# Swapping two VectorE instructions at the end of the output phase: the next attention's second scaling ahead of the last gated product

## The chip, the cores and the metric

The kernel runs on one core of a Trainium2 chip. The metric is device time in microseconds (us). PE is TensorE (matmul), DVE is VectorE, ACT is ScalarE, POOL is GpSimd, SP issues DMAs. Each engine has an instruction queue of its own; engines wait for each other through semaphores.

## The reference

Eight batches of linear attention (8 heads, 576 tokens, head dimension 64) are followed by a gated feed-forward layer over all 4608 tokens (model width 512, hidden width 1536):

```
kv  = k^T v                      # per head, 64 x 64
o   = q kv
x   = o / sqrt(mean(o*o) + 1e-6) * g_norm          # heads side by side: 512 wide
hid = gelu(x @ w_gate) * (x @ w_val)               # 1536 wide
out = x + sigmoid(x @ w_res) * (hid @ w_out)
```

## The kernel before

Tokens are worked through in nine blocks. Blocks 0 to 7 hold 512 tokens of one batch each; block 8 holds the 64 remaining tokens of each of the eight batches. A block has a **gate/value phase** (`x @ w_gate`, `x @ w_val`, GELU, product) and an **output phase** (`hid @ w_out`, sigmoid gate, sum with x). The attention of batch `b` is computed inside the phases of earlier blocks: for b = 3 to 7 its raw output o is made and scaled across the output phase of block b-2 and the gate/value phase of block b-1. So what is "next" in the output phase of block m is the attention of batch m+2.

There is no scheduler. Every engine executes in the order in which the Python code issues its instructions. Two tables place the attention's pieces between the feed-forward's: `amid_gv` (pieces behind a given word of the gate/value order) and `amid_out` (pieces at a given place of the output phase, called by `aside(key)`).

**The output phase.** Large products are cut into quadrants and computed with seven products in place of eight (Strassen-Winograd), so each phase is a chain of seven matrix products with sums between them. In `others()` of `out_by_products` the last five products are issued by `prod` (L518, 12 matmuls each) into the PSUM banks w_A, w_E, w_A, w_F, w_A. `sub` (L481) makes the sums on DVE. `pf` (L701) multiplies a finished quarter by its gate into the result tile `osb`: the quarter from w_E, the one from w_F, the one that was set aside (on POOL), and last the one from w_A. That last `pf((1, 0), w["A"])` is the **last gated product**; it is the last reader of the bank w_A.

**The scaling.** `a_t(b, i)` (L348) multiplies part i of the raw attention output (a PSUM bank `op`) by the inverse norms `ny` and writes the fp16 tile `t`. It is the last reader of that `op` bank. There are four such parts per batch. Part 0 is placed at key "11" (at "01" in block 1), ahead of the last gated product; part 1, the **second scaling**, is the first item of `aside("end")`. For blocks 2 to 5 it is the only item there; for block 1 two sums over tokens (`ts`, L481, third and fourth of `token_sums`) follow it. Parts 2 and 3 are placed behind the words 1v and Fv of the following gate/value group (in block 2's group: Fv and cv). All of this is on DVE.

**The gate/value phase that follows.** `gv_group` works through a string of words. The first group of blocks 2 to 6 uses

```
1g 1v Eg 5g 6g Ev 5v dg 6v dv Fg 2g Fv 2v 7g g11 7v cg 3g cv 3v h11 g12 4g g21 h12 4v g22 h21 h22
```

A digit is a product on PE (L949, 4 matmuls), g for the gate and v for the value side. Products 1, 6, 7 and 4 go into the bank A of their side, 5 and 3 into F, 2 into E. `E` (`seed`, L959, ACT) copies A, as product 1 left it, into bank E. `d` (`keep`, L963, ACT) copies F, as product 5 left it, to SBUF. `F` and `c` (`plus`, L970, DVE) add d to A. `g11` and the like are GELUs (L980, ACT), `h11` and the like the products with the value side (L986, DVE, for 22 POOL). In the second group of a block the order is `1g 1v Eg 5g Ev 5v dg 6g dv 6v Fg 2g Fv 2v 7g ...`.

**Who holds which bank.** `banks_of` assigns the eight PSUM banks. In the first group of the next block, bank E of the value side (Ev) is the bank that was w_A, so the seed `Ev` waits for the last gated product. Bank F of the gate side (5g) is the bank of part 0 of the attention output; bank F of the value side (5v) is the bank of part 1, so product 5v waits for the second scaling. Within the group: 6v overwrites what the seed `Ev` reads, so it waits for that copy; 7g and 7v write onto A behind 6g and 6v, so they wait for the DVE sums `Fg` and `Fv`, which read A; 4g and 4v wait likewise for `cg` and `cv`.

Of the kernel before, what the change touches and what calls it, by code (L numbers as in the profile page):

```python
# [18 lines left out]
def kernel(  # L19
# [343 lines left out]
    def row_times_g(blk, jj, eng):  # L363
        eng.tensor_tensor(out=t_t[blk][:, jj, :], in0=t_t[blk][:, jj, :], in1=g16, op=ALU.mult)  # L364
# [109 lines left out]
    def b_of(i, j):  # L474
        return wo16[:, (i - 1) * NFH : i * NFH, (j - 1) * CH : j * CH]

    def a_of(blk, i, j):
        return hids[blk][:, (j - 1) * NFH : j * NFH, (i - 1) * PR : i * PR]

    def sub(eng, out_, in0, in1, op=ALU.subtract):  # L480
        eng.tensor_tensor(out=out_, in0=in0, in1=in1, op=op)  # L481
# [29 lines left out]
    def s_last(blk):  # L511
        sub(nc.vector, hid_sums[3], a_of(blk, 1, 2), hid_sums[1])

    def prod(ps, a, b, start, es=(0, 1)):

        for e in es:
            for f in range(NFH):
                nc.tensor.matmul(  # L518
                    ps[:, e - es[0], :],
                    lhsT=a[:, f, e * P : (e + 1) * P],  # L520
                    rhs=b[:, f, :],
                    start=(start and e == es[0] and f == 0),
                    stop=(f == NFH - 1),
                    skip_group_check=True,
                )
# [76 lines left out]
    def res_and_attn(blk):  # L602
        return WHOLE <= blk and blk + 2 < B
# [4 lines left out]
    def out_by_products(blk, banks, amid):  # L608
# [3 lines left out]
        def aside(ahead_of):  # L612
            for f in amid.get(ahead_of, ()):
                f()
# [82 lines left out]
        def part(jj):  # L697
            return slice(None), slice(2 * jj[0], 2 * jj[0] + 2), slice(jj[1] * CH, (jj[1] + 1) * CH)

        def pf(jj, src, eng=nc.vector):  # L700
            eng.tensor_tensor(out=res_all[part(jj)], in0=th_all[part(jj)], in1=src, op=ALU.mult)  # L701
# [10 lines left out]
        def others():  # L712


            prod(w["A"], s_[1], wo_t[:, 1], False)
            aside("F")
            sub(nc.vector, w["F"], w["A"], w["d"], ALU.add)
            if res_and_attn(blk):
                s_last(blk)
            aside("00")  # L720
            prod(w["E"], a_of(blk, 1, 2), b_of(2, 1), False)
            if not whole(blk + 1):
                pf((0, 0), w["E"])
            aside("22")
            prod(w["A"], s_[2], wo_t[:, 2], False)
            c22 = res_all[part((1, 1))]
            sub(nc.vector, c22, w["A"], w["d"], ALU.add)
            if whole(blk + 1):
                pf((0, 0), w["E"])
            aside("01")  # L730
            prod(w["F"], s_[3], b_of(2, 2), False)
            pf((0, 1), w["F"])
            aside("11")
            prod(w["A"], a_of(blk, 2, 2), wo_t[:, 3], False)
            if whole(blk + 1):
                pf((1, 1), c22, nc.gpsimd)
                pf((1, 0), w["A"])
                aside("end")
            else:
                pf((1, 1), c22)  # L740
                pf((1, 0), w["A"])
            if blk + 1 == WHOLE or blk + 1 == LAST[0]:
                nc.gpsimd.tensor_copy(out=hold, in_=x_sums[blk + 1][0:1, 3, 1, 1, 0:1])
            if blk == LAST[0]:
                nc.gpsimd.tensor_copy(out=hold, in_=s_[3][0:1, 0, 0:1])
            for j in range(NJ):
                row_times_g(blk, j, nc.gpsimd)
            if blk == LAST[0]:
                for p in range(B // 2):
                    row_times_g(B, p, nc.gpsimd)  # L750
            rows_behind()

        def rows_behind():

            for i in (1, 0):
                at_word(blk + 1, 0, "h22", lambda i=i: fin((i, i)), lambda i=i: fin((i, 1 - i)))
                at_word(blk + 1, 1, "h22", lambda i=i: store(i))
# [637 lines left out]
    def whole(blk):  # L1395

        return WHOLE <= blk < B - 1
# [249 lines left out]
```

## Time and profile before

| | us |
|---|---|
| median of three runs (lowest to highest) | 320.42 (320.38 to 320.46) |
| span of the profiled execution, first to last instruction | 319.6 |
| PE busy | 309.5 |
| DVE busy | 275.2 |
| ACT busy | 210.8 |
| POOL busy | 188.0 |

The page gives only the span of the profiled execution; the median lies 0.8 us above it, and a change of the span is read as a change of the time. The granted PE clock is full in all 40 slices (mean 0.999). A matmul is shown with a modelled duration of 0.27 us, while the next one starts 0.109 us later, so four matmuls of a product appear as 0.60 us and the next product starts after 0.44 us. DVE and ACT instructions that follow each other without a wait overlap a little in the record: a 0.68 us DVE instruction is followed after 0.60 us, a 0.57 us ACT copy after 0.49 us. Times in the trace are microseconds from the span's start. The output phases of blocks 1 to 5 end, on PE, near 92.0, 124.4, 156.9, 189.4 and 222.2 us.

### The profile page before, as it was taken

How to read it: one execution, taken by the hardware profiler on the slowest of the kernel's cores; microseconds unless marked ns; L12 is line 12 of the kernel's file. 1: busy time of each engine (PE TensorE's matmuls, PEld its weight loads, DVE VectorE, ACT ScalarE, POOL GpSimd, SP SyncE). 2: the span in 40 equal slices, each digit the busy share in tenths (PEclk: the TensorE clock that was granted, in tenths of full speed). 3: DMA queues.
4: the chain of work that ended last, by engine and by line, in shares of the span. 5: the costliest groups of instructions: out<-in, count | busy, mean ns of one | idle time of the engine just before them, and what ended most of it. 6: DMA issues, size and time to landing. Idle time of an engine off the chain costs nothing.

```text
span 319.6 us, 7753 instructions
## 1 busy us (share of the span) xinstructions
PE 309.5 (97%) x3039; PEld 245.6 (77%) x3039; DVE 275.2 (86%) x488; ACT 210.8 (66%) x385; POOL 188.0 (59%) x248
## 2 busy tenths in 40 slices
PE   7899989999999999999999999999999999999993
PEld 2544755444788888888888888888888888888882
DVE  5886979799898999989998999899988777897774
ACT  4763675456848794879587858795767467736770
POOL 2873350573769479756875887517761375396332
PEclk9999999999999999999999999999999999999999
DMA  7999999799994699479947694800340003000204
GB/s 253 328 192 202 195 203 196 162 153 189 171 118 82 199 138 97 82 216 128 105 84 215 88 145 71 226 6 0 68 148 2 0 3 132 2 2 40 93 0 131
DMA packets 77253, 38.89 MB, mean 122 GB/s; under 512 B 42146, under 2 KB 74914, under 8 KB 77218
## 3 DMA queue, kind: packets, MB, share of 16 engines
q0 software_dynamic: 39280, 17.17, 42.7%
q1 hardware_dynamic: 37360, 20.71, 24.8%
q10 hardware_dynamic: 578, 0.52, 0.5%
q8 instruction: 23, 0.38, 0.5%
q14 instruction: 12, 0.10, 0.1%
HBM read 38.80 MB, written 9.44 MB: 151 GB/s over the span
## 4 chain that ended last, share of the span: by engine, by line
PE 84%; DMA 11%; SPq 1%; POOL 1%; DVE 1%; issue 0%; DVEq 0%
PE Ag L949 12%; PE Av L949 11%; PE wA L518 11%; PE Fv L949 6%; PE Fg L949 6%; DMA wg<-in_moe_w_gate_dram 5%; DMA wo<-in_moe_w_out_dram 5%; PE rA L569 4%; PE gps L413 3%; PE fps L450 3%; PE vps L413 3%; PE Ev L949 3%; PE Eg L949 3%; PE wD L518 3%; PE wF L518 3%; PE wE L518 3%
## 5 line engine op out<-in xcount | busy, mean ns | idle before, releaser
L986 POOL TENSOR_TENSOR hid<-ge,c 128x512 f16<-128x512 f16 x22 | 25.6, 1164 | 37.9 <-ACT ge L980 37.9
L518 PEld LDWEIGHTS <-hid_s 128*128 128x128 f16 x384 | 37.6, 98 | 4.4
L949 PEld LDWEIGHTS <-wsv 128*128 128x128 f16 x352 | 34.1, 98 | 5.2 <-issue 1.1
L949 PEld LDWEIGHTS <-wsg 128*128 128x128 f16 x352 | 34.4, 98 | 4.0
L364 POOL TENSOR_TENSOR t<-t,g 128x512 f16<-128x512 f16 x32 | 37.1, 1188 | 0.0
L705 POOL TENSOR_TENSOR osb<-osb,t 128x512 f32<-128x512 f32 x28 | 34.1, 1246 | 0.0
L959 ACT COPY Eg<-Ag 128x512 f32<-128x512 f32 x22 | 12.8, 584 | 27.9 <-PE Ag L949 27.9
L518 PEld LDWEIGHTS <-hid 128*128 128x128 f16 x288 | 28.2, 98 | 3.5
L949 PEld LDWEIGHTS <-wg 128*128 128x128 f16 x264 | 25.8, 98 | 3.2
L949 PEld LDWEIGHTS <-wv 128*128 128x128 f16 x264 | 25.8, 98 | 3.0
L949 PE MATMUL Av<-ts,wsv 128*128 128x256 f16 x176 | 26.4, 272 | 0.1
L949 PE MATMUL Ag<-ts,wsg 128*128 128x256 f16 x176 | 26.4, 273 | 0.0
L970 DVE TENSOR_TENSOR Fg<-Ag,d 128x512 f32<-128x512 f32 x22 | 15.3, 697 | 11.0 <-ACT d L963 8.1
L261 DVE TENSOR_REDUCE ss<-sq 128x8 f32<-128x512 f32 x32 | 20.5, 679 | 2.4 <-ACT sq L256 2.4
L401 ACT ACTIVATE ge<-gps 128x512 f16<-128x512 f32 x20 | 11.9, 598 | 15.6 <-PE gps L413 13.6
L518 PE MATMUL wA<-wo_ts,hid_s 128*128 128x256 f16 x168 | 20.6, 273 | 0.0
L980 ACT ACTIVATE ge<-Eg 128x512 f16<-128x512 f32 x22 | 13.2, 598 | 9.9 <-PE Eg L949 9.9
L980 ACT ACTIVATE ge<-c 128x512 f16<-128x512 f32 x22 | 13.8, 627 | 7.7 <-DVE c L970 7.7
L413 PE MATMUL vps<-xT,wv 128*128 128x512 f16 x72 | 18.5, 379 | 0.4 <-DMA wv<-in_moe_w_val_dram 0.3
L348 DVE TENSOR_TENSOR t<-op,ny 128x512 f16<-128x512 f32 x28 | 18.4, 684 | 0.5 <-POOL ny L322 0.4
L970 DVE TENSOR_TENSOR c<-Ag,d 128x512 f32<-128x512 f32 x22 | 15.2, 689 | 3.9 <-PE Ag L949 3.8
L413 PE MATMUL gps<-xT,wg 128*128 128x512 f16 x72 | 18.5, 379 | 0.0
(220 smaller groups left out, 851.0 us busy)
## 6 DMA issues: line engine op xcount, KB each, us to landing
out_dram<-osb SPq DMA_DIRECT2D x14, 512.0 KB, 3.4
qraw<-in_q_dram POOLq DMA_DIRECT2D x7, 512.0 KB, 6.5
k<-in_k_dram POOLq DMA_DIRECT2D x7, 512.0 KB, 8.4
v<-in_v_dram POOLq DMA_DIRECT2D x7, 512.0 KB, 10.4
wg<-in_moe_w_gate_dram POOLq DMA_DIRECT2D x2, 512.0 KB, 9.5
wo<-in_moe_w_out_dram POOLq DMA_DIRECT2D x2, 512.0 KB, 13.6
out_dram<-osb SPq DMA_DIRECT2D x4, 256.0 KB, 3.8
wv<-in_moe_w_val_dram POOLq DMA_DIRECT2D x3, 256.0 KB, 8.5
```

Source lines behind the costliest of these rows:

```text
L261: nc.vector.tensor_reduce(out=out_, in_=sqs.pop((b, i)), op=ALU.add, axis=mybir.AxisListType.X)
L348: nc.vector.tensor_tensor(out=t, in0=o, in1=scale, op=ALU.mult)
L364: eng.tensor_tensor(out=t_t[blk][:, jj, :], in0=t_t[blk][:, jj, :], in1=g16, op=ALU.mult)
L413: nc.tensor.matmul(ps[:, j0 * P : j1 * P], lhsT=w[:, cc, :], rhs=xT_t[blk][:, j0:j1, cc, :], start=(cc == 0 and j0 == 0), stop=(cc == NP - ...
L518: nc.tensor.matmul(ps[:, e - es[0], :], lhsT=a[:, f, e * P : (e + 1) * P], rhs=b[:, f, :], start=(start and e == es[0] and f == 0), stop=( ...
L569: nc.tensor.matmul(out_[:, e, :], lhsT=x_[:, e, cc, :], rhs=w_[:, cc, :], start=(first and e == 0 and cc == 0), stop=(cc == 1), skip_group ...
L705: nc.gpsimd.tensor_tensor(out=res_all[of], in0=res_all[of], in1=t_t[blk][of], op=ALU.add)
L949: nc.tensor.matmul(out_[:, r, :], lhsT=lhsT, rhs=rhs, start=(first and r == 0 and c == 0), stop=(c == 1), skip_group_check=True,)
L959: nc.scalar.copy(out=tile_of("E", u), in_=ps["A", u])
L970: nc.vector.tensor_tensor(out=dst, in0=ps["A", u], in1=sb["d", u], op=ALU.add)
L980: nc.scalar.activation(out=ge[q], in_=source(q, "g"), func=AF.Gelu)
L986: eng.tensor_tensor(out=dst, in0=ge[q], in1=source(q, "v"), op=ALU.mult)
```

## The change

In `others()`, the branch for blocks whose next block is one of 2 to 6, `aside("end")` is moved ahead of the last gated product:

```
             if whole(blk + 1):
                 pf((1, 1), c22, nc.gpsimd)
+                aside("end")
                 pf((1, 0), w["A"])
-                aside("end")
             else:
```

The branch is taken in the output phases of blocks 1 to 5. DVE's order there becomes, for blocks 2 to 5, scaling 0, scaling 1, gated product of w_A, scaling 2 (before: scaling 0, gated product, scaling 1, scaling 2). For block 1 it becomes gated product of w_F, scaling 1, two `ts` sums, gated product of w_A (before: gated products of w_F and w_A, scaling 1, two `ts` sums). No instruction is added or removed, and the order on PE, ACT, POOL and SP is the same in both kernels. Product 2v of the following group gets a semaphore wait of its own for the gated product; before, that was already covered by the wait of product 5v. A few waits for POOL move to a neighbouring GELU on ACT.

More of the change, by code (lines that the diff above doesn't have):

```diff
@@ L736, in others @@
                 pf((1, 1), c22, nc.gpsimd)
+                aside("end")
                 pf((1, 0), w["A"])
-                aside("end")
             else:
```

## The prediction

> **What bounds the kernel now.** I read the page's busy times first, then the chain of work that ended last, then the waits of each engine, then the timeline of all engines from 124.3 to 130.7 us, where block 2's output phase ends and block 3's gate/value phase starts.
>
> ```profile
> PE 309.5 (97%) x3039; PEld 245.6 (77%) x3039; DVE 275.2 (86%) x488; ACT 210.8 (66%) x385; POOL 188.0 (59%) x248
> PE 84%; DMA 11%; SPq 1%; POOL 1%; DVE 1%; issue 0%; DVEq 0%
> ```
>
> PE bounds it, and behind the opening the chain stays on PE product after product: whatever delays PE between 90 and 230 us delays the end by as much, and nothing behind it waits for another engine long enough to give that back. In the waits of ACT the row that matters is the seed Ev waiting for the gated product.
>
> ```profile
> ACT Ev L959 <- DVE osb L701: 0.5, 3, 0.2
> ```
>
> Now the timeline (start, duration, engine, instruction, idle time before it).
>
> ```profile
> 124.35 0.69 DVE L348 TENSOR_TENSOR t<-op,ny 128x512 f16<-128x512 f32 x1
> 124.96 0.68 DVE L701 TENSOR_TENSOR osb<-th,wA 128x512 f32<-128x512 f32 x1
> 124.99 0.57 ACT L959 COPY Eg<-Ag 128x512 f32<-128x512 f32 x1 [3.54 <-PE Ag L949]
> 125.23 0.60 PE L949 MATMUL Fg<-ts,wsg 128*128 128x256 f16 x4
> 125.55 1.28 DVE L348 TENSOR_TENSOR t<-op,ny 128x512 f16<-128x512 f32 x2
> 125.67 0.60 PE L949 MATMUL Ag<-ts,wsg 128*128 128x256 f16 x4
> 125.72 0.57 ACT L959 COPY Ev<-Av 128x512 f32<-128x512 f32 x1 [0.16 <-DVE osb L701]
> 126.21 0.59 ACT L963 COPY d<-Fg 128x512 f32<-128x512 f32 x1
> 126.29 0.60 PE L949 MATMUL Fv<-ts,wsv 128*128 128x256 f16 x4
> 126.72 0.60 PE L949 MATMUL Av<-ts,wsv 128*128 128x256 f16 x4
> 126.83 0.70 DVE L970 TENSOR_TENSOR Fg<-Ag,d 128x512 f32<-128x512 f32 x1
> 126.92 0.59 ACT L963 COPY d<-Fv 128x512 f32<-128x512 f32 x1
> 127.54 0.70 DVE L970 TENSOR_TENSOR Fv<-Av,d 128x512 f32<-128x512 f32 x1
> 128.03 0.60 PE L949 MATMUL Ag<-ts,wsg 128*128 128x256 f16 x4
> 128.47 0.60 PE L949 MATMUL Av<-ts,wsv 128*128 128x256 f16 x4
> ...
> ```
>
> Three things are to be seen. Product 5v (Fv, 126.29) starts 0.62 us after 6g (125.67) instead of 0.44: it waits for the second scaling, 125.55 + 0.68 = 126.23, so PE loses 0.18 us. DVE runs back to back from 124.35 to 127.5; the product of w_A ended long before DVE came to it (124.14 + 0.38 = 124.52 against 124.96), so moving it fills no idle DVE time, it only trades places. And ACT waits for the gated product before Ev (124.96 + 0.68 = 125.64, Ev at 125.72), with both d copies queued behind Ev, and DVE's Fg and Fv behind the d copies (126.21 + 0.59 = 126.80, Fg at 126.83).
>
> **The change part by part: blocks 2 to 5.** The four boundaries repeat within 0.02 us (Ev at 125.72, 158.26, 190.79 and 223.57), so one is worked and counted four times. Steps used: DVE to the next DVE 0.60; ACT copy to the next 0.49; DVE end to ACT start 0.08 (125.64 to 125.72); ACT end to DVE start 0.03; DVE end to PE start 0.06 (126.23 to 126.29); product to product 0.44.
>
> The second scaling goes to 124.96 and ends at 125.64. Product 5v can start at its own pace, 126.10: 0.18 us won, all of it on PE.
>
> The gated product goes to 125.55 and ends at 126.23. Ev therefore runs 126.31 to 126.88 (now 125.72 to 126.29). No row shows a hand-over from ACT to PE; its nearest rows are 0.06 (DVE to PE) and 0.03 to 0.08 (DVE with ACT), I take 0.06. Product 6v, which overwrites what Ev reads, starts at 126.94 instead of its own pace 126.54: 0.40 lost, against now (126.72) 0.22. Within 0.05 this hand-over decides nothing below.
>
> The d copies follow at 126.80 and 127.28, ending 127.39 and 127.87. Scaling 2 keeps its slot (126.15). DVE's Fg starts at 127.42 instead of 126.83, after 0.6 us of DVE idle; Fv at 128.02 instead of 127.54 (+0.48). Product 7g at its own pace is 128.25 and Fg ends at 128.12: no wait. Product 7v at its own pace is 128.69; Fv ends at 128.70, so 7v starts at 128.76 (now 128.47: +0.29). DVE then runs scaling 3 at 128.62, cg 129.22, cv 129.82 to 130.50; product 4v at its own pace is 130.51, with the hand-over 130.56 (now 130.22: +0.34).
>
> DVE has no idle time to make up its 0.48 before the second group: it is back to back up to that group's Fv, because the remainder's scaling sits there. The row of that Fv and of the 7v behind it, from the timeline of 133.5 to 135:
>
> ```profile
> 133.84 0.68 DVE L970 TENSOR_TENSOR Fv<-Av,d 128x512 f32<-128x512 f32 x1
> 134.58 0.60 PE L949 MATMUL Av<-ts,wsv 128*128 128x256 f16 x4
> 134.78 0.69 DVE L970 TENSOR_TENSOR c<-Ag,d 128x512 f32<-128x512 f32 x1 [0.26 <-PE Ag L949]
> ```
>
> Fv ends at 134.52 and 7v starts 0.06 later: no slack beyond the hand-over. With DVE 0.48 late PE is 0.48 late there. Behind it DVE waits 0.26 us for 7g (and 0.60 us in the third group), so it catches up and nothing more is lost. Sum per boundary: +0.48 us, the 0.18 won already in it. Times four: **+1.92 us**.
>
> **Block 1.** Here three instructions pass the gated product, from the timeline of 91.9 to 99:
>
> ```profile
> 92.42 0.68 DVE L701 TENSOR_TENSOR osb<-th,wA 128x512 f32<-128x512 f32 x1
> 93.01 0.69 DVE L348 TENSOR_TENSOR t<-op,ny 128x512 f16<-128x512 f32 x1
> 93.19 0.57 ACT L959 COPY Ev<-Av 128x512 f32<-128x512 f32 x1
> 93.61 0.42 DVE L481 TENSOR_TENSOR ts<-xT 128x512 f16<-128x512 f16 x1
> ```
>
> Scaling and two sums take 0.60 + 0.34 + 0.34 = 1.28 us, so the gated product runs 93.70 to 94.38. Ev moves from 93.19 to 94.46 and ends at 95.03; 6v moves from 94.19 to 95.09 (+0.90). The d copies end at 95.54 and 96.03, Fg starts at 95.57 (now 94.30), Fv at 96.17 and ends at 96.85. 7v at its own pace would be 96.83, with Fv 96.91 (now 95.93: +0.98). Scaling 2, cg, cv follow; cv ends at 98.65, 4v starts at 98.71 (now 97.68: +1.03). The next group has no remainder scaling and DVE idles 0.64 us before its Fg, so the loss stays **+1.03 us**. Product 5v waited only 0.03 here, so nearly nothing is won. POOL's copy `hold`, which waits for the second ts sum, and the four products by g behind it go 0.6 us earlier; POOL's hid22 follows ACT's GELU, so this is costed at nothing.
>
> **Other queues passed.** The gated product's result is read by POOL's sums at word h22, near 132.7, some 6 us later: hidden. Scaling 3 is 0.5 us later (1.1 in block 1), and SP's transposing DMA with it (issued 128.90, 2.4 to 4.2 us to landing); its reader runs at 136.0, so 2.9 us cover it. The new wait of product 2v is for the gated product, which ends at 126.23 while 2v runs near 127.8: nothing. The instructions keep their durations.
>
> **Sum.** 1.92 + 1.03 = 2.95 us. The profiled span of 319.6 becomes 322.6; the median lies 0.8 above, so 320.42 becomes **323.4**.
>
> **Two rules weighed.** The page "Perfetto Trace Analysis" of the Trainium skill (Optimization Strategy) says to find the gaps of the bound engine and make what it waits for start sooner. The gap at 5v is such a gap, and by that rule alone the change would bring 4 x 0.18 + 0.03 = 0.75 us. The rows speak against stopping there, since the instruction passed feeds the same engine 1 us later. The page "PSUM — Partial Sum Buffer" (Engine vs sequencer instructions) says that ScalarE's queue is strictly first in, first out. The row agrees in this case: 5g ended at 125.83, yet d ran only at 126.21, behind Ev. If ACT could take d first, only the 6v loss would remain, 0.22 x 4 + 0.90 = 1.78 us in place of 2.95.
>
> **Rivals.**
> *Only 6v pays* (DVE makes up its lateness before the 7v products, as it would if the d copies were not held or DVE spaced tighter than 0.60): 0.22 x 4 + 0.90 = 1.78, that is 322.2. For it: 7g has slack and 7v misses by only 0.07 in the first group. Against it: DVE has no wait from 127.54 to 134.52.
> *The lateness adds up* (DVE's whole 0.59 at Ev reaches PE, and the 0.18 is not won as well because another wait holds 5v): 4 x (0.59 + 0.18) + 1.28 = 4.36, that is 324.8. For it: ACT and DVE each hand on the full 0.59 to the next. Against it: 7g has slack, and ACT reorders nothing that 5v needs.
> *Faster*: the 0.18 per block is won and Ev's lateness is hidden: 4 x 0.18 and block 1's 0.03 make 0.75, and 320.42 - 0.75 = 319.7. It decides if Ev is at most 0.19 us later than now: Ev would have to end by 126.48 for 6v at 126.54 to keep its pace, against the expected 0.59. The one mechanism is that the moved scaling costs DVE at most 0.19 us ahead of the gated product. Every row has 0.60 for it; only if the gated product could start while the scaling drains would it come near.
> *Nothing happens* (Ev did not hang on the gated product): the wait row names it three times, so it has little for it.
>
> **How the numbers follow.** The first case with its own range 322.8 (the second group's 7v costs nothing: 4 x 0.34 + 1.03 = 2.39) to 323.9 (4 x 0.59 + 1.1) has 0.60. Only 6v: 0.18. Adds up: 0.14. Faster: 0.05. No change: 0.03. A measurement of this kernel tells 0.2% (0.64 us) from nothing. The range must leave out no more than 0.2: it takes in the first case, the second and the third with their edges, 321.7 to 324.8. Slower 0.92, same 0.03, faster 0.05.
>
> **What would show it.** In the changed kernel's profile: 5v 0.44 behind 6g; Ev idle some 0.7 us for the gated product in blocks 2 to 5 and longer in block 1; a gap of 0.4 us before 6v; DVE idle 0.6 us before Fg, released by d; small gaps before 7v in the first and second group; block 2 to block 3 on PE 33.0 us apart instead of 32.5. Wrong would be: a 6v without a gap, or a 7v in the second group that keeps pace, or losses of block 1 no larger than those of the others.

## The result

The changed kernel takes 322.74 us (median of six), the kernel before 320.5. The ratio is 1.0067, with a 95% interval of 1.0048 to 1.0086, or 2.1 us (1.5 to 2.8). Run a second time, against the kernel before in the same series, it was 1.0074 (1.0045 to 1.0103), 2.4 us (1.4 to 3.3). The change makes the kernel slower by 0.7%. The forecast was 323.4, a loss of 2.95 us: above the first interval and inside the second, so the times alone don't settle by how much it was off; the phases below do.

The execution behind the first trace of the changed kernel was a slow one (331.3 us, with a pause of 7 us in a late block that no other trace shows) and isn't part of the ratio, so all lines below are from the second run's trace (span 321.3 us). Its page, and the wait of PE that is new:

```profile
PE 311.1 (97%) x3039; PEld 246.2 (77%) x3039; DVE 273.9 (85%) x488; ACT 209.9 (65%) x385; POOL 187.7 (58%) x248
PE 83%; DMA 11%; DVE 1%; SPq 1%; POOL 1%; ACT 1%; issue 1%; DVEq 0%; ACTq 0%
```

```profile
PE Av L949 <- ACT Ev L959: 1.7, 5, 0.8
```

PE is the bound as before, and now waits five times, once per changed boundary, for the seed Ev on ACT: 0.76 us in block 1 and about 0.23 in each of the others. (These count from the modelled end of the product before; from start to start the delay is larger, as the next lines show.) The timeline at the end of block 2's output phase (start, duration, engine, instruction, idle before it):

```profile
124.51 1.29 DVE L348 TENSOR_TENSOR t<-op,ny 128x512 f16<-128x512 f32 x2
124.53 0.60 PE L949 MATMUL Ag<-xT,wg 128*128 128x256 f16 x4
...
125.72 0.68 DVE L701 TENSOR_TENSOR osb<-th,wA 128x512 f32<-128x512 f32 x1
125.84 0.60 PE L949 MATMUL Ag<-ts,wsg 128*128 128x256 f16 x4
126.28 0.60 PE L949 MATMUL Fv<-ts,wsv 128*128 128x256 f16 x4
...
126.48 0.57 ACT L959 COPY Ev<-Av 128x512 f32<-128x512 f32 x1 [0.74 <-PE Ag L949]
126.96 0.59 ACT L963 COPY d<-Fg 128x512 f32<-128x512 f32 x1
127.10 0.60 PE L949 MATMUL Av<-ts,wsv 128*128 128x256 f16 x4 [0.23 <-ACT Ev L959]
...
127.59 0.70 DVE L970 TENSOR_TENSOR Fg<-Ag,d 128x512 f32<-128x512 f32 x1 [0.59 <-ACT d L963]
...
128.20 0.69 DVE L970 TENSOR_TENSOR Fv<-Av,d 128x512 f32<-128x512 f32 x1
...
128.41 0.60 PE L949 MATMUL Ag<-ts,wsg 128*128 128x256 f16 x4
...
128.94 0.60 PE L949 MATMUL Av<-ts,wsv 128*128 128x256 f16 x4
```

Product 5v (126.28) follows 6g (125.84) after 0.44: its wait is gone. The gated product ends at 126.40 and Ev starts 0.08 later. The trace puts this wait down to PE's Ag, whose product 6g ends at 126.44; but Ev doesn't need 6g: in the kernel before it starts at 125.72, when 6g has just begun (125.67). Product 6v comes 0.82 after 5v instead of 0.44. DVE idles 0.59 us before Fg, and 7v (128.94) comes 0.53 after 7g. What was won at 5v is lost, and more, at 6v, 7v and 4v.

The clearest measure is PE's own phase length: the time from the first product of one block's gate/value phase to that of the next, read from the PE timelines (column "1" is the phase that begins after block 1's output phase). Where two kernels have the same order it repeats within some hundredths of a microsecond, while whole runs of one kernel differ by up to 2.9 us (the kernel before: 319.9 to 322.75).

| kernel | 1 | 2 | 3 | 4 | 5 | sum | against before |
|---|---|---|---|---|---|---|---|
| before | 32.39 | 32.53 | 32.54 | 32.78 | 30.74 | 160.98 | |
| changed, second run | 33.40 | 32.87 | 32.87 | 33.11 | 31.08 | 163.33 | +2.35 |
| blocks_2_5 | 32.38 | 32.87 | 32.87 | 33.11 | 31.07 | 162.30 | +1.32 |
| swap_2_5 | 32.38 | 32.52 | 32.53 | 32.76 | 30.73 | 160.92 | -0.06 |
| swap_alone | 32.39 | 32.87 | 32.87 | 33.12 | 31.08 | 162.33 | +1.35 |
| scaling_only | 32.72 | 32.87 | 32.88 | 33.11 | 31.08 | 162.66 | +1.68 |
| keep_first | 33.23 | 32.80 | 32.80 | 33.05 | 31.01 | 162.89 | +1.91 |
| pool_held | 33.41 | 32.86 | 32.88 | 33.18 | 31.08 | 163.41 | +2.43 |
| copied | 32.51 | 32.36 | 32.37 | 32.60 | 30.58 | 160.42 | -0.56 |
| copied_2_5 | 32.40 | 32.36 | 32.37 | 32.61 | 30.57 | 160.31 | -0.67 |

The changed kernel loses 1.01 us in phase 1 and 0.34, 0.33, 0.33 and 0.34 in the others: 2.35 us, which is inside both intervals of the times.

### The profile page after: what moved, and what is told of

The parts are those of the page before. It is cut to its first block, busy times and chain, and to the rows that moved or that the text cites. A ratio compares the mean times of both kernels' runs of the same rounds, so it can differ in the third digit from the quotient of the medians.

```text
span 329.5 us, 7753 instructions
## 1 busy us (share of the span) xinstructions
PE 311.9 (95%) x3039; PEld 247.0 (75%) x3039; DVE 278.6 (85%) x488; ACT 210.0 (64%) x385; POOL 186.4 (57%) x248
## 4 chain that ended last, share of the span: by engine, by line
PE 81%; DMA 10%; DVE 4%; SPq 1%; POOL 1%; ACT 1%; issue 1%; DVEq 0%; ACTq 0%
PE Av L949 12%; PE Ag L949 11%; PE wA L518 11%; PE Fg L949 5%; PE Fv L949 5%; DMA wo<-in_moe_w_out_dram 5%; DMA wg<-in_moe_w_gate_dram 4%; PE rA L569 4%; PE gps L413 3%; PE fps L450 3%; PE vps L413 3%; PE wE L518 3%; PE Ev L949 3%; PE Eg L949 3%; PE wD L518 3%; DVE ts L481 2%
## 5 line engine op out<-in xcount | busy, mean ns | idle before, releaser
L949 PEld LDWEIGHTS <-wsv 128*128 128x128 f16 x352 | 34.0, 98 | 7.2 <-issue 2.5
L949 PEld LDWEIGHTS <-wsg 128*128 128x128 f16 x352 | 34.4, 98 | 4.0
L364 POOL TENSOR_TENSOR t<-t,g 128x512 f16<-128x512 f16 x32 | 35.9, 1150 | 0.0
L959 ACT COPY Eg<-Ag 128x512 f32<-128x512 f32 x22 | 12.8, 582 | 35.5 <-PE Ag L949 35.5
L949 PEld LDWEIGHTS <-wg 128*128 128x128 f16 x264 | 26.0, 99 | 3.4
L949 PEld LDWEIGHTS <-wv 128*128 128x128 f16 x264 | 25.9, 98 | 3.3
L949 PE MATMUL Av<-ts,wsv 128*128 128x256 f16 x176 | 26.4, 272 | 1.6 <-ACT Ev L959 1.6
L949 PE MATMUL Ag<-ts,wsg 128*128 128x256 f16 x176 | 26.4, 273 | 0.0
```

The source lines that it names most:

```text
L949: nc.tensor.matmul(out_[:, r, :], lhsT=lhsT, rhs=rhs, start=(first and r == 0 and c == 0), stop=(c == 1), skip_group_check=True,)
L959: nc.scalar.copy(out=tile_of("E", u), in_=ps["A", u])
```

## The experiments

**The changed kernel again.**

> The changed kernel as it is, for a trace without the pause of 7 us that the first one has in a later block. Bank theory (the delayed release of Ev's bank costs PE what it costs up to the end of the first group, and the second group adds nothing): 1.00 us for block 1 and 0.33 for each of blocks 2 to 5, 2.3 us in all, output phase to output phase 32.86 us on PE for blocks 2 to 4 instead of 32.53. Carry theory (as predicted: VectorE brings its 0.48 us into the second group, where PE pays it): 2.95 us in all, 33.0 us from phase to phase.

323.24 us, ratio 1.0074 (1.0045 to 1.0103); phases 33.40 and 32.87. The second group adds nothing; the carry theory falls, and the section "Why the prediction was right, and where it was off" says why.

**blocks_2_5: the change without block 1.** (`WHOLE` is 2.)

```
+                if blk >= WHOLE:
+                    aside("end")
                 pf((1, 0), w["A"])
-                aside("end")
+                if not (blk >= WHOLE):
+                    aside("end")
```

> The change in the output phases of blocks 2 to 5 alone; block 1 as before. Bank theory: 4 x 0.33 = 1.3 us above the kernel before. Carry theory: 4 x 0.48 = 1.9 us. If block 1 made the whole loss: nothing.

322.11 us, ratio 1.0038 (1.0021 to 1.0055), 1.2 us; phase 1 is as before, the others as in the changed kernel. The parts add up: block 1 is 1.0 us, the other four together 1.3.

**swap_2_5 and swap_alone: who waits for which bank.** Both trade two banks in the first group of blocks 3 to 6. The first has the changed order in blocks 2 to 5, the second the order of before everywhere.

```
+        if blk > WHOLE and whole(blk):
+            g0 = groups[0]
+            g0["v", "E"], g0["v", "F"] = g0["v", "F"], g0["v", "E"]
         return groups
```

The output of both kernels is not the reference's (relative error 0.05); why is not shown, so they serve for timing alone. Apart from the two banks, the instructions and their sizes are the same.

> As blocks_2_5, but in the first group of blocks 3 to 6 the value side's banks E and F trade places, so that the seed Ev waits for the second scaling and product 5v for the gated product. VectorE has the changed order. Bank theory: what is released second is again what 5v waits for, so all is as before: within 0.2 us of the kernel before, phase to phase 32.53. Order theory (what costs is that VectorE runs the gated product later or the scaling earlier, whoever waits for it): 1.3 us above, as blocks_2_5.

> The kernel before with VectorE's old order in every block, and only the same two banks traded in the first groups of blocks 3 to 6. Bank theory: Ev now hangs on the second scaling, which ends 0.59 us after the gated product, so the loss of the change appears without the change: 4 x 0.33 = 1.3 us above the kernel before, product 6v some 0.4 us behind its pace. Order theory: as the kernel before, within 0.2 us.

swap_2_5 takes 320.49 us, ratio 0.9991 (0.9971 to 1.0011): the changed DVE order costs nothing when Ev no longer hangs on the instruction that comes second. swap_alone takes 322.21 us, ratio 1.0038 (1.0018 to 1.0058): the loss of the change without the change. From swap_alone's timeline, at the same boundary:

```profile
124.31 0.68 DVE L701 TENSOR_TENSOR osb<-th,wA 128x512 f32<-128x512 f32 x1
...
124.91 1.28 DVE L348 TENSOR_TENSOR t<-op,ny 128x512 f16<-128x512 f32 x2
...
125.68 0.57 ACT L959 COPY Ev<-Av 128x512 f32<-128x512 f32 x1 [0.75 <-PE Ag L949]
...
126.30 0.60 PE L949 MATMUL Av<-ts,wsv 128*128 128x256 f16 x4 [0.23 <-ACT Ev L959]
```

and from swap_2_5's (whose added lines move L959 and L949 to L962 and L952):

```profile
124.76 0.68 DVE L701 TENSOR_TENSOR osb<-th,wA 128x512 f32<-128x512 f32 x1
...
124.93 0.57 ACT L962 COPY Ev<-Av 128x512 f32<-128x512 f32 x1 [0.15 <-DVE t L348]
...
125.49 0.60 PE L952 MATMUL Fv<-ts,wsv 128*128 128x256 f16 x4
125.92 0.60 PE L952 MATMUL Av<-ts,wsv 128*128 128x256 f16 x4
```

In the first, Ev waits for the second scaling (124.91 + 0.68 = 125.59; the trace again names PE's Ag) with DVE in its old order, and 6v waits the same 0.23 us as in the changed kernel. In the second, Ev goes at once behind the scaling, and 5v is the one that is late, as in the kernel before. So the order theory falls: which of the two DVE runs first doesn't set the time by itself; what does is whether Ev or 5v gets its bank second. 5v has 0.18 us to lose; Ev has a chain behind it.

**scaling_only: block 1 without the sums.** In block 1 the two `ts` sums stay behind the gated product.

```
                 pf((1, 1), c22, nc.gpsimd)
-                aside("end")
+                at_end = amid["end"]
+                at_end[0]()
                 pf((1, 0), w["A"])
+                for f in at_end[1:]:
+                    f()
```

> In block 1 the two ts sums stay behind the gated product, and only the second scaling goes ahead of it, as in blocks 2 to 5. Bank theory: block 1 costs what the 0.60 us of one scaling cost, worked by the same steps: 0.3 us instead of 1.0, phase 1 to phase 2 32.7 us on PE (before 32.39, changed kernel 33.39); 5 x 0.33 = 1.65 us in all. Were block 1 dear for another reason (its bank of 5v, POOL's wait for the sums), it would stay near 33.4.

Phase 1 is 32.72 us, as worked out; the phases' sum is 1.68 us above before, against 1.65 expected. Ev waits 0.61 us for DVE there instead of 1.28. From the changed kernel's timeline, and then from scaling_only's:

```profile
93.62 0.57 ACT L959 COPY Ev<-Av 128x512 f32<-128x512 f32 x1 [1.28 <-DVE osb L701]
94.24 0.60 PE L949 MATMUL Av<-ts,wsv 128*128 128x256 f16 x4 [0.76 <-ACT Ev L959]
```

```profile
92.78 0.57 ACT L962 COPY Ev<-Av 128x512 f32<-128x512 f32 x1 [0.61 <-DVE osb L701]
```

So block 1's extra 0.68 us (33.40 - 32.72) is the time of the two sums. The times alone (ratio 1.0077, 1.0049 to 1.0106) don't separate this kernel from the changed one.

**keep_first: ACT's queue.**

```
-        None: "1g 1v Eg 5g 6g Ev 5v dg 6v dv Fg ...
+        None: "1g 1v Eg 5g 6g dg Ev 5v 6v dv Fg ...
```

> The changed kernel with one more edit: in the first group of blocks 2 to 6 ScalarE copies d of the gate side ahead of the seed Ev. If the d copies behind Ev, and VectorE's idle time before Fg, set the loss, it falls to what 5v won against little, 0 to 0.1 per block. If product 6v sets it, which overwrites what Ev reads, VectorE's idle time of 0.60 us before Fg goes, but 6v still waits 0.2 to 0.3 us, and the loss is 0.26 per block in place of 0.33 and 0.9 in place of 1.0 in block 1: 1.95 us in all.

Ratio 1.0072 (1.0051 to 1.0092); the phases lose 0.27 each in blocks 2 to 5 and 0.84 in block 1, 1.91 in all. From its timeline:

```profile
126.33 0.59 ACT L963 COPY d<-Fg 128x512 f32<-128x512 f32 x1 [0.30 <-PE Fg L949]
...
126.81 0.59 ACT L959 COPY Ev<-Av 128x512 f32<-128x512 f32 x1
127.20 0.69 DVE L970 TENSOR_TENSOR Fg<-Ag,d 128x512 f32<-128x512 f32 x1
...
127.45 0.60 PE L949 MATMUL Av<-ts,wsv 128*128 128x256 f16 x4 [0.29 <-ACT Ev L959]
```

With d ahead of Ev, DVE's idle time before Fg is gone, yet 6v still waits 0.29 us, and that wait is now the whole loss: counted from the phase's first product, 6v starts at 2.63, against 2.36 in the kernel before, and no later product of the phase falls further behind. In the changed kernel 6v starts at 2.57, so 0.21 of its loss of 0.34 arises at 6v and the other 0.13 at 7v and 4v, behind the queued d copies. keep_first takes off the 0.13, but Ev, now behind a copy, delays 6v by 0.06 more: a gain of 0.07.

**pool_held: what the remainder's scaling waits for.** POOL's product hid22 is held until DVE's `t<-o` is done: a copy of one element on POOL, ahead of hid22, reads `t`.

```
-    at_word(m + 1, 0, "h21", lambda: a_t(b, NJ), lambda: d_xT(b, NJ, NJ + 1))
+    at_word(m + 1, 0, "h21", lambda: a_t(b, NJ), lambda: d_xT(b, NJ, NJ + 1), lambda: nc.gpsimd.tensor_copy(out=hold, in_=t_t[B][0:1, pair(b), 0:1]))
```

> The changed kernel, with GpSimd's product hid22 of the first group held back (blocks 3 to 6) until the remainder's scaling t<-o on VectorE is done. If t<-o is stretched by the GpSimd product that runs beside it (in every block it ends 0.59 us after that product), it takes 0.7 us in place of 1.14 and follows at VectorE's pace, and hid22 starts about 1 us later. If 1.1 to 1.3 us are its own cost, it stays. In both cases PE's phases stay at 32.87 us, within 0.1, since 7v of the second group has no wait there in the changed kernel.

From its timeline, in block 4:

```profile
166.55 0.68 DVE L348 TENSOR_TENSOR t<-o,ny 128x512 f16<-128x512 f32 x1
...
167.30 0.18 POOL L1448 COPY hold<-t 1x1 f16<-1x1 f16 x1 [3.24 <-DVE t L348]
167.44 1.16 POOL L986 TENSOR_TENSOR hid<-ge,c 128x512 f16<-128x512 f16 x1
167.52 0.70 DVE L970 TENSOR_TENSOR Fg<-Ag,d 128x512 f32<-128x512 f32 x1 [0.29 <-PE Ag L949]
```

`t<-o` (the scaling of the remainder, the block-8 tokens) takes 0.68 us alone, and follows at DVE's pace. In the kernel before it took 1.33 there, in the changed one 1.14. hid22 starts 1.5 us later in the phase, where about 1 was expected. The phases stay as in the changed kernel within 0.1. The whole time, 325.08 us, is that of a single run and is not compared.

**copied and copied_2_5: a version that keeps both in time.** DVE keeps the order of before without the gated product: ACT, idle then, copies w_A to the result tile, and POOL makes the product.

```
                 pf((1, 1), c22, nc.gpsimd)
-                pf((1, 0), w["A"])
+                c21 = res_all[part((1, 0))]
+                nc.scalar.copy(out=c21, in_=w["A"])
+                pf((1, 0), c21, nc.gpsimd)
                 aside("end")
```

> Old order of the scalings, but in blocks 1 to 5 ScalarE, idle for 3.5 us ahead of Eg, copies w_A to the result tile, and GpSimd makes the gated product from there. VectorE loses 0.60 us of work between the two scalings, so the second scaling ends at 125.6 and Ev waits for ScalarE's own copy alone. Bank theory: 5v and 6v keep pace, 0.18 us won in each of blocks 2 to 5 and 0.03 in block 1: 0.75 us faster than the kernel before, phase to phase 32.35. Against it: GpSimd has 1.27 us more per block; if its rows by g push hid22, and with it the remainder's scaling, 7v of the second group waits, and the gain shrinks to 0 to 0.3 us or turns to a loss of up to 1.

> As copied, but block 1 keeps the kernel before's order: there GpSimd's added product ran beside VectorE's first ts sum, which took 1.40 us instead of 0.42, and that phase became 0.12 us longer. If that was the whole of block 1's loss, phase 1 to phase 2 goes back to 32.39 us on PE, the others stay at 32.36, and the kernel is 0.68 us faster than before (0.2%, at the edge of what the times tell). If the added work on GpSimd costs elsewhere, the times show no gain though the phases are shorter.

copied: 320.32 us, ratio 1.0003 (0.9983 to 1.0023): in the times nothing of the expected 0.75 us shows. The phases 2 to 5 are 0.16 to 0.18 us shorter, as worked out, but phase 1 is 0.12 longer. There DVE's first `ts` sum runs beside POOL's added product:

```profile
92.17 1.27 POOL L701 TENSOR_TENSOR osb<-th,osb 128x512 f32<-128x512 f32 x1 [0.46 <-ACT osb L738]
92.32 1.40 DVE L481 TENSOR_TENSOR ts<-xT 128x512 f16<-128x512 f16 x1
```

copied_2_5: 320.50 us, ratio 0.9994 (0.9975 to 1.0014). Phase 1 is back at 32.40, so the 0.12 came from block 1's edit (that it came from the longer sum is likely, not shown), and the phases' sum is 0.67 us below before. That is the gain expected, but in the times it is too small to be told from nothing: the phases are shorter in the trace, and a faster kernel is not shown.

## Why the prediction was right, and where it was off

The place, the sign and the mechanism up to the end of the first group held; the term for the second group did not. Measured from the first product of the phase, the changed kernel runs as the steps had it, but for the last point:

- **5v** keeps pace: 0.18 us won in blocks 2 to 5. Right.
- **Ev** follows the gated product by 0.08 and **6v** follows Ev by 0.05 (126.48 + 0.57 = 127.05, 6v at 127.10; 0.06 assumed). Right.
- **DVE idle before Fg, Fv late by 0.5, 7v of the first group late.** Right: 7v comes 0.53 after 7g where 0.51 was worked out, and the first group's end was to be 0.34 late; the second group starts 0.33 late and phase 2 is 0.34 longer.
- **Block 1**: +1.03 forecast, 1.01 measured. Right, and scaling_only shows that the two sums make its surplus.
- **The second group**, "With DVE 0.48 late PE is 0.48 late there": wrong. PE is 0.33 late when that group starts and still 0.33 late at its 7v. That step overstated the loss by 0.14 us four times, 0.56 in all; without it the sum is 2.95 - 0.56 = 2.39, and the phases show 2.35. The step read "back to back" as "busy": it took DVE's row `t<-o` as work of 1.33 us that starts when DVE comes to it. From the kernel before and the changed one, the second group of block 4:

```profile
164.15 1.16 POOL L986 TENSOR_TENSOR hid<-ge,c 128x512 f16<-128x512 f16 x1 [1.61 <-ACT ge L980]
164.53 1.33 DVE L348 TENSOR_TENSOR t<-o,ny 128x512 f16<-128x512 f32 x1
165.27 2.72 POOL L705 TENSOR_TENSOR osb<-osb,t 128x512 f32<-128x512 f32 x2
```

```profile
164.94 1.16 POOL L986 TENSOR_TENSOR hid<-ge,c 128x512 f16<-128x512 f16 x1 [1.92 <-ACT ge L980]
165.51 1.14 DVE L348 TENSOR_TENSOR t<-o,ny 128x512 f16<-128x512 f32 x1
166.07 2.73 POOL L705 TENSOR_TENSOR osb<-osb,t 128x512 f32<-128x512 f32 x2
...
167.18 0.68 DVE L970 TENSOR_TENSOR Fv<-Av,d 128x512 f32<-128x512 f32 x1
167.96 0.60 PE L949 MATMUL Av<-ts,wsv 128*128 128x256 f16 x4
```

`t<-o` ends 0.59 us after POOL turns from hid22 to its next instruction, in both (164.53 + 1.33 - 165.27; 165.51 + 1.14 - 166.07, to 0.01). Its end hangs on POOL, which follows ACT's GELU and was only 0.28 us late (164.94 - 157.40 against 164.15 - 156.89). DVE came 0.48 late and had 0.19 less to wait inside the instruction; Fv then ended at 167.86, and 7v kept its pace at 167.96. pool_held shows the cause: without POOL beside it the instruction takes 0.68 us. The lines quoted in the prediction don't show it: they leave out POOL's rows and the stretch from 131 to 133 us, where block 3's `t<-o` runs.

One of the three signs that the prediction gave for being wrong thus did appear, a 7v of the second group that keeps pace; the other two did not. The loss measured is the lower edge of the first case (322.8, "the second group's 7v costs nothing"). The whole range, 321.7 to 324.8, also took in "only 6v pays" (322.2), so that the times fell inside it says little: the phases are what tells the two apart. And that the second run's 323.24 lies close to 323.4 is in part chance, since the kernel before read 320.75 in that series and not 320.42.

The rival "only 6v pays" had the right reason in part (DVE makes up its lateness), but too early: 7v and 4v of the first group do pay, 0.13 us together. "The lateness adds up" failed on both its terms: 5v did win its 0.18, and 7g has no wait. The "faster" rival failed by the condition given for it: the gated product starts 0.59 us later in the phase (125.72 - 124.53 against 124.96 - 124.36), not 0.19. Of the two rules weighed, filling the gap of the bound engine did what it says (5v keeps pace) and was still a loss. For the order within ACT's queue keep_first gives the number: taking d first gains 0.07 per block and 0.17 in block 1, 0.44 us in all (2.35 - 1.91). The prediction had 1.17 for it (2.95 - 1.78): 0.56 of that is the second group's term, and the other 0.61 left out that Ev, behind a d copy, comes later.

## What to carry to other kernels

Before two instructions on a busy engine trade places, follow both results to the bound engine and compare the slack of each: here the one had 0.18 us to win, and the other had a copy, a bank overwrite and two sums behind it. An engine without gaps in its row is not an engine without slack: an instruction whose duration differs between calls of one shape may hold a wait inside it, and its end should be read against what runs on the other engines. Where an effect is below the scatter of the times, the distance between two equal points of the bound engine's timeline shows it.

## What the runs showed of the hardware

In these traces a DVE instruction with two inputs in SBUF that starts while POOL is at work on a 128x512 product from SBUF takes longer, as if it stood still until that product is nearly over. `t<-o` took 0.68 us alone and 1.14 to 1.65 when hid22 had begun before it, always ending about 0.59 us after POOL turned to its next instruction; a `ts` sum took 0.41 us alone and 1.40 when it started 0.15 us behind POOL's product. POOL pays as well: the product that it starts while `t<-o` finishes took 1.60 us, against 1.15 in pool_held, where `t<-o` is out of the way. DVE's scalings with one input in PSUM kept 0.68 to 0.69 us beside POOL's products by g. The page "SBUF — State Buffer" of the Trainium skill (Who interferes with whom) has this rule: a VectorE instruction with two SBUF inputs contends with a GpSimd instruction that reads SBUF. These rows agree. With POOL's rows beside it, it would have hung the second group's step on the end of hid22, and the forecast would have been some 322.8 (an estimate: 320.42 + 2.39).
